# Linear attention and a two-layer feed-forward on one core: an earlier release for batch 1's loads, two tokens' transposes begun sooner, batch 2's exponentials placed behind more activations

## The chip, the cores and the metric

The kernel runs on one core of a Trainium2 chip. The metric is the device time of one execution in microseconds; times of several runs are given as a median. A profiled execution has a time of its own, and its span is the stretch from its first to its last instruction.

A core has TensorE (PE; its weight loads are shown as PEld), VectorE (DVE), ScalarE (ACT), GpSimd (POOL) and SyncE (SP), each running its own instructions in order and waiting on semaphores. SP issues most of the transfers, POOL the ones that change the type, and 16 DMA engines move the data of all queues. In the profile q1 is the queue fed by SP and q0 the one fed by POOL.

## The reference

```python
def _attn_ref(q, k, v):                       # 8 batches, 8 heads, 576 tokens, 64 wide
    q_s = exp(q - max(q, axis=-1)); q_s = q_s / sum(q_s, axis=-1)
    k_s = exp(k - max(k, axis=2));  k_s = k_s / sum(k_s, axis=2)
    kv = einsum('bhsd,bhse->bhde', k_s, v)
    return einsum('bhsd,bhde->bhse', q_s, kv)

x = attn_out.transpose(0, 2, 1, 3).reshape(4608, 512)
h = x @ w_in                                  # 512 x 2048
out = maximum(0.01 * h, h) @ w_out            # 2048 x 512, float32
```

## The kernel before

**Layout.** The attention of each batch is prepared on 128 partitions: heads come in two halves (`H0`, `H1`), and each partition holds nine rows (`R = 9`) of 64 values for each of four head pairs. For `k` the maximum over all tokens is taken on VectorE (`k_tree`, `k_allmax`), subtracted (`k_sub`) and exponentiated on ScalarE (`k_exp`); for `q` a maximum per row (`q_max`), a subtraction (`q_sub`), an exponential (`q_exp`), a sum (`q_sum`) and a scaling (`q_norm`). `v_cast` puts `v` into bfloat16. `kv` multiplies keys and values on TensorE, first heads of gg = 0, then of gg = 1; `kd_make` scales the result into a block-diagonal tile. The scaled `q` is turned, for batch 0 by transposes on TensorE (`q_transpose`, copied out by `q_keep`), for later batches by a DMA (`q_turn`, issued on SP). `attend` or `attend_x` multiplies the turned `q` with the `kd` tile, and a copy puts the product into `xT`, the input of the feed-forward.

**The feed-forward** runs over nine tiles of 512 tokens. For each of 16 column blocks j, `layer1` makes four matmuls into a PSUM tile `ph`, over the column blocks 0, 2, 1, 3 of `w_in` in this order, and `leaky` (ScalarE, line 470) writes the activation into `g_sb`. Then `layer2` (line 482) sums 16 matmuls for each of four groups of 128 tokens into `pout`, and `store` copies and sends it. Tile 0 takes 576 tokens instead of 512 and is split further. Its first 256 tokens come in halves: `begin(j)` makes the matmuls with column blocks 0 and 2 for j and j + 1, and line 682 the ones with 1 and 3; the remaining 320 tokens follow in one loop, and tile 0's `layer2` goes with j outermost, four token groups for each j. Six PSUM banks (`psB`) are handed out in turn to `ph`, `po`, `pkv`, `psum_qt` and others.

**Order.** All instruction streams are in the order of the program text. Preparation of later batches is put between matmuls by hand: `at(t, u, ...)` files functions under tile t and step u, and `run(t, u)` emits them there. In tile t ≥ 1 step j comes behind the `leaky` of block j (0 to 15), and steps 16 and up come behind every fourth matmul of `layer2`. `plan2` places batch 2 in tile 1 (lines 623 to 638), `plan` the later ones.

**Loads.** `w_in` comes in two halves of columns. Each is four DMAs on POOL's queue, in the order (gg, hp): gg chooses column blocks {0, 2} or {1, 3}, hp the partitions 0 to 63 or 64 to 127. `w_out` follows in six DMAs, also on POOL's queue, behind a gate: the copy on line 579 reads an element of the first half of batch 1's `k`, so POOL goes on only when that has landed. `k`, `q` and `v` of batch 1 are issued on SP (lines 576 to 578), and they are held: `hold_sync` (line 513) issues a small DMA on SP that reads some elements of `w_in_sb`, and SP doesn't come to the loads behind it before the transfer that writes these elements has landed. The elements lie in partition 64, column block 0, last 128 columns.

Of the kernel before, what the change touches and what calls it, by code (L numbers as in the profile page):

```python
# [25 lines left out]
def kernel(  # L26
# [9 lines left out]
    nc = tc.nc  # L36
# [3 lines left out]
    B, H, S, D = q.shape  # L40
    C = H * D
    T = B * S
    Cm, F = moe_w_in.shape
# [28 lines left out]
    def load(src, b, name, cuts):  # L72

        t = raw_pool.tile([P, HL, R, D], FP32, name=name, tag="raw")
        flat = src[b].rearrange("h s d -> (h s d)").rearrange(
            "(hl p r d) -> p hl r d", hl=HL, p=P, r=R
        )
        for hs, rs in cuts:
            nc.sync.dma_start(
                out=t[:, hs, rs].rearrange("p h r d -> p h (r d)"),  # L80
                in_=flat[:, hs, rs].rearrange("p h r d -> p h (r d)"),
            )
        return t

    ALLH, ALLR = slice(0, HL), slice(0, R)
# [28 lines left out]
    w_in_sb = w_pool.tile([P, NB, F], BF16)  # L114
# [29 lines left out]
    def k_begin(b):  # L144
        st[b]["ke"] = ke_pool.tile([P, R, HL, D], BF16, name="ke")
        st[b]["kmax"] = mx_pool.tile([P, HL, D], FP32, name="kmax")
        st[b]["kmaxT"] = mx_pool.tile([P, HL * D], FP32, name="kmaxT")
        st[b]["kall"] = mx_pool.tile([P, HL, D], FP32, name="kall")

    def k_tree(b, hs, steps=slice(0, 4)):  # L150
        n = hs.stop - hs.start
        ks = st[b]["k"][:, hs]
        if steps.start == 0:
            st[b]["t4"] = mx_pool.tile([P, HL, 4, D], FP32, name="t4")[:, 0:n]
        t4 = st[b]["t4"]
        t2, t1 = t4[:, :, 0:2], t4[:, :, 0]
        for o, i0, i1 in (
            (t4, ks[:, :, 0:4], ks[:, :, 4:8]),
            (t2, t2, t4[:, :, 2:4]),
            (t1, t1, t4[:, :, 1]),  # L160
            (st[b]["kmax"][:, hs], t1, ks[:, :, 8]),
        )[steps]:
            nc.vector.tensor_tensor(out=o, in0=i0, in1=i1, op=ALU.max)  # L163

    def k_allmax(b):


        nc.vector.transpose(
            out=st[b]["kmaxT"], in_=st[b]["kmax"].rearrange("p h d -> p (h d)")
        )  # L170
        m2 = small_pool.tile([P, CB, 2], FP32, name="m2")
        nc.vector.tensor_reduce(
            out=m2[:, :, 0],
            in_=st[b]["kmaxT"].rearrange("p (c j) -> p c j", j=32),
            axis=AX.X,
            op=ALU.max,
        )
        for a in range(4):
            o = a ^ 1
            nc.vector.tensor_reduce(  # L180
                out=m2[32 * o : 32 * o + 32, :, 1],
                in_=m2[32 * a : 32 * a + 32, :, 0:1],
                axis=AX.X,
                op=ALU.max,
            )
        m = small_pool.tile([P, CB], FP32, name="m")
        nc.vector.tensor_reduce(out=m, in_=m2, axis=AX.X, op=ALU.max)
        nc.vector.transpose(  # L188
            out=st[b]["kall"].rearrange("p h d -> p (h d)"),
            in_=m.unsqueeze(2).to_broadcast([P, CB, 32]),  # L190
        )

    def k_sub(eng, b, hs):
        ks = st[b]["k"][:, hs]
        n = hs.stop - hs.start
        eng.tensor_tensor(  # L196
            out=ks,
            in0=ks,
            in1=st[b]["kall"][:, hs].unsqueeze(2).to_broadcast([P, n, R, D]),
            op=ALU.subtract,  # L200
        )

    def k_exp(b, hs):
        nc.scalar.activation(  # L204
            out=st[b]["ke"][:, :, hs].rearrange("p r h d -> p h r d"),
            in_=st[b]["k"][:, hs],
            func=AF.Exp,
        )
# [10 lines left out]
    def q_begin(b):  # L219
        st[b]["qe"] = qe_pool.tile([P, R, HL, D], BF16, name="qe")  # L220
        if b == 0:
            for gg in range(2):
                st[b]["qT", gg] = qT_pool.tile([P, 2, R, L], BF16, name=f"qT{gg}", tag="qT")
# [42 lines left out]
    def q_exp(b, rs):  # L266
        nc.scalar.activation(  # L267
            out=st[b]["qe"][:, rs].rearrange("p r h d -> p h r d"),
            in_=st[b]["q"][:, :, rs],
            func=AF.Exp,  # L270
        )

    def q_sum(b, rs):
        n = rs.stop - rs.start
        qsum = small_pool.tile([P, n, HL], FP32, name="qsum")
        nc.vector.reduce_sum(out=qsum, in_=st[b]["qe"][:, rs], axis=AX.X)  # L276
        st[b]["qrec", rs.start] = qrec = small_pool.tile([P, n, HL], FP32, name="qrec")
        nc.vector.reciprocal(out=qrec, in_=qsum)

    def q_norm(b, rs):  # L280
        n = rs.stop - rs.start
        qes = st[b]["qe"][:, rs]
        nc.vector.tensor_tensor(  # L283
            out=qes,
            in0=qes,
            in1=st[b]["qrec", rs.start].unsqueeze(3).to_broadcast([P, n, HL, D]),
            op=ALU.mult,
        )
# [104 lines left out]
    def q_transpose(b, r0, n):  # L393
        ps = psB_pool.tile([P, NB, n, L], BF16, name="psum_qt", tag=BANK_TAG)
        for rr in range(n):
            for gg in range(2):
                nc.tensor.matmul(
                    ps[:, gg::2, rr],
                    lhsT=st[b]["qe"][:, r0 + rr, 2 * gg : 2 * gg + 2].rearrange(
                        "p h d -> p (h d)"  # L400
                    ),
                    rhs=ident,
                    is_transpose=True,
                    start=(rr == 0 and gg == 0),
                    stop=(rr == n - 1 and gg == 1),
                )
        st[b]["ps", r0] = ps

    def q_keep(eng, b, r0, n, ggs=(0, 1)):
        for gg in ggs:  # L410
            o, i = st[b]["qT", gg][:, :, r0 : r0 + n], st[b]["ps", r0][:, gg::2]
            if eng is nc.scalar:
                eng.copy(out=o, in_=i)
            else:
                eng.tensor_copy(out=o, in_=i)
# [20 lines left out]
    def q_turn(b, rs=ALLR):  # L436
        if rs.start == 0:
            st[b]["qX"] = qT_pool.tile([P, R * 2, P], BF16, name="qX", tag="qT")
        nc.sync.dma_start_transpose(
            out=st[b]["qX"][:, 2 * rs.start : 2 * rs.stop],  # L440
            in_=st[b]["qe"][:, rs].rearrange("p r h d -> p (r h d)"),
        )
# [50 lines left out]
    def at(t, u, *fns):  # L493
        while t > 0 and u >= 32:
            t, u = t + 1, u - 32
        hooks.setdefault((t, u), []).extend(fns)
# [16 lines left out]
    def hold_sync(i, src):  # L513
        nc.sync.dma_start(out=held[:, i], in_=src)
# [57 lines left out]
    q_norm(0, R1)  # L572


    hold_sync(0, w_in_sb[D : D + 1, 0, F - 128 : F])
    st[1]["k"] = load(k, 1, "k_raw", [(H0, ALLR), (H1, ALLR)])
    st[1]["q"] = load(q, 1, "q_raw", [(ALLH, ALLR)])
    st[1]["v"] = load(v, 1, "v_raw", [(ALLH, ALLR)])
# [44 lines left out]
    def plan2():  # L623
        b = 2
        at(1, 0, lambda: k_begin(b), lambda: q_begin(b), lambda: k_tree(b, ALLH))
        at(1, 3, lambda: k_allmax(b))
        at(1, 6, lambda: k_sub(nc.vector, b, H0), lambda: k_sub(nc.vector, b, H1))
        at(1, 9, lambda: k_exp(b, ALLH))
        for rs in XR:
            at(1, 9, lambda rs=rs: q_max(b, rs), lambda rs=rs: q_sub(nc.gpsimd, b, rs))  # L630
        at(1, 13, lambda: v_cast(nc.gpsimd, b, 0), lambda: v_cast(nc.gpsimd, b, 1))
        for i, rs in enumerate(XR):
            at(1, (13, 16)[i], lambda rs=rs: q_exp(b, rs), lambda rs=rs: q_sum(b, rs), lambda rs=rs: q_norm(b, rs))
            at(1, (15, 17)[i], lambda rs=rs: q_turn(b, rs))
        at(1, 21, lambda: kv(b))
        at(1, 22, lambda: kd_make(b))
        for i in range(8):
            at(1, 28 + i // 2, lambda i=i: attend_x(b, i % 4, XR[i // 4], nc.scalar))
# [20 lines left out]
    def begin(j):  # L659
        ph = psB_pool.tile([P, 2, 256], FP32, name="ph", tag=BANK_TAG)  # L660
        for i in range(2):
            layer1(j + i, ph[:, i], 0, 256, slice(0, 2), i == 0)
        begun.append(ph)
# [7 lines left out]
    q_norm(0, R2)  # L671
    for j in range(0, NF, 2):
        if j == 8:
            for jj in range(8, NF, 2):
                begin(jj)
            q_transpose(0, 4, 2)
            q_transpose(0, 6, 3)
            q_keep(nc.vector, 0, 4, 2)
            q_keep(nc.vector, 0, 6, 3)
        ph = begun.pop(0)  # L680
        for i in range(2):
            layer1(j + i, ph[:, i], 0, 256, slice(2, 4), i == 0, i == 1)
            if i == 1:
                leaky(g_sb[j // 2][:, :, 0:256], ph)
            run(0, j + i)
# [72 lines left out]
```

## Time and profile before

| | |
|---|---|
| median of 3 runs | 292.64 us (292.42 to 292.85) |
| profiled execution | 292.92 us |
| its span | 291.1 us |
| TensorE busy | 278.7 us, 96% of the span |
| VectorE, ScalarE, GpSimd busy | 148.5, 147.9, 86.0 us |
| granted TensorE clock | 1.000 |
| data moved by DMA | 46.35 MB |
| the held DMA's issue on SP | 21.07 us |
| tile 0's last `layer1` matmul ends, its `layer2` begins | 34.88 us, 35.55 us |

The busy time of an engine is the union of its instructions; for TensorE matmuls overlap each other in their records, since they are pipelined, and a gap between two records is shorter than the time that was lost. A timeline row gives start, duration, engine, line, operation and tiles of instructions of one kind in a row, and in brackets the idle time before them with what ended it. Issues of a DMA are listed with the time from issue to landing. Rows of a DMA queue give packets, megabytes and the time that its packets took as a share of 16 engines.

### The profile page before, as it was taken

Reading aid. Unit: us, or ns where it says so; the run is one execution under the profiler, and the core shown is the slowest. Engines: PE = TensorE matmul, PEld = TensorE weight load, DVE = VectorE, ACT = ScalarE, POOL = GpSimd, SP = SyncE. Lnnn points to the kernel's source line nnn. Section 1 sums busy time; section 2 is a strip of 40 time slices with the busy share of each in tenths; the row PEclk is TensorE's granted clock in tenths of the full one; section 3 lists DMA queues with packets and bytes.
Section 4 is the critical chain, followed back from the end, with each engine's and each line's share of the span. In section 5 each row is a group of like instructions: output and inputs, shape, how many; then the busy total and the mean of one; then the engine's idle time right before and its main releaser. Section 6 shows DMA issues by size and latency. Waiting matters only on the chain.

```text
span 291.1 us, 4248 instructions
## 1 busy us (share of the span) xinstructions
PE 278.7 (96%) x1620; PEld 138.5 (48%) x1646; DVE 148.5 (51%) x246; ACT 147.9 (51%) x273; POOL 86.0 (30%) x70
## 2 busy tenths in 40 slices
PE   8689899998999999999999999999999999999995
PEld 3268644453444445454444444554455444444443
DVE  3997693796890796289275546645541200110011
ACT  4976870658168506941684339533953066017400
POOL 4734560008039108603910391029200000000000
PEclk9999999999999999999999999999999999999999
DMA  7998999998649365963298139913141310131033
GB/s 258 311 205 302 282 194 212 398 283 312 130 94 360 133 125 108 372 173 85 68 351 233 36 73 330 275 36 72 38 81 36 74 36 1 36 77 34 0 70 76
DMA packets 38932, 46.35 MB, mean 159 GB/s; under 512 B 18304, under 2 KB 21632, under 8 KB 38912
## 3 DMA queue, kind: packets, MB, share of 16 engines
q1 hardware_dynamic: 35456, 41.75, 48.7%
q0 software_dynamic: 3296, 4.20, 8.3%
q8 instruction: 13, 0.21, 0.3%
q10 hardware_dynamic: 160, 0.13, 0.1%
q14 instruction: 7, 0.06, 0.1%
HBM read 36.70 MB, written 9.44 MB: 158 GB/s over the span
## 4 chain that ended last, share of the span: by engine, by line
PE 74%; issue 1%; ACT 0%; DVE 0%; ACTq 0%
PE pout L482 37%; PE ph L461 33%; PE pkv L298 2%; PE po L449 2%; ACT gj L470 0%; ACT xT L455 0%; DVE out_sb L476 0%; ACTq L470 0%
## 5 line engine op out<-in xcount | busy, mean ns | idle before, releaser
L482 PE MATMUL pout<-w_out_sb,gj 128*128 128x512 bf16 (+2 forms) x580 | 129.1, 373 | 2.9 <-DMA w_out_sb<-in_moe_w_out_dram 1.1
L461 PE MATMUL ph<-xT,w_in_sb 128*128 128x512 bf16 (+3 forms) x627 | 126.8, 357 | 1.9 <-DMA w_in_sb<-in_moe_w_in_dram 0.7
L470 ACT ACTIVATE gj<-ph 128x512 bf16<-128x512 f32 (+2 forms) x152 | 83.3, 581 | 56.8 <-PE ph L461 54.9
L461 PEld LDWEIGHTS <-w_in_sb 128*128 128x128 bf16 x640 | 62.2, 98 | 63.4 <-issue 2.3
L482 PEld LDWEIGHTS <-gj 128*128 128x128 bf16 x592 | 56.9, 98 | 65.4 <-issue 3.1
L476 DVE COPY out_sb<-pout 128x512 f32<-128x512 f32 (+1 forms) x34 | 22.7, 675 | 86.1 <-PE pout L482 82.6
L196 POOL TENSOR_TENSOR k_raw<-k_raw,kall 128x2304 f32<-128x2304 f32 x5 | 25.3, 5070 | 77.5 <-DVE kall L188 50.4
L455 ACT CAST xT<-po 128x320 bf16<-128x320 f32 (+1 forms) x54 | 18.8, 405 | 49.4 <-PE po L449 49.4
L259 POOL TENSOR_TENSOR q_raw<-q_raw,qmax 128x2304 f32<-128x2304 f32 (+3 forms) x10 | 29.7, 2977 | 23.3 <-DVE qmax L228 23.3
L276 DVE TENSOR_REDUCE qsum<-qe 128x36 f32<-128x2304 bf16 (+4 forms) x11 | 19.8, 1797 | 30.9 <-ACT qe L267 30.9
L204 ACT ACTIVATE ke<-k_raw 128x2304 bf16<-128x2304 f32 (+2 forms) x11 | 17.6, 1596 | 11.2 <-POOL k_raw L196 8.6
L283 DVE TENSOR_TENSOR qe<-qe,qrec 128x2304 bf16<-128x2304 bf16 (+4 forms) x12 | 21.9, 1826 | 0.4
L228 DVE TENSOR_REDUCE qmax<-q_raw 128x36 f32<-128x2304 f32 (+4 forms) x11 | 19.6, 1789 | 1.9 <-DMA q_raw<-in_q_dram 1.9
L267 ACT ACTIVATE qe<-q_raw 128x2304 bf16<-128x2304 f32 (+4 forms) x11 | 16.8, 1526 | 0.6 <-POOL q_raw L259 0.3
L216 POOL CAST vb<-v_raw 128x1152 bf16<-128x1152 f32 x13 | 14.6, 1153 | 0.0
L449 PE MATMUL po<-qX,kd 128*128 128x320 bf16 (+1 forms) x56 | 11.6, 286 | 0.3
L327 PE MATMUL pout<-zero 128*128 128x512 bf16 x27 | 9.2, 478 | 1.3 <-POOL zero L101 1.3
L163 DVE TENSOR_TENSOR t<-k_raw 128x1024 f32<-128x1024 f32 (+1 forms) x10 | 10.1, 1011 | 0.5 <-DMA k_raw<-in_k_dram 0.2
L163 DVE TENSOR_TENSOR t<-t 128x256 f32<-128x256 f32 (+2 forms) x20 | 9.6, 478 | 0.6
L476 ACT COPY out_sb<-pout 128x512 f32<-128x512 f32 (+1 forms) x3 | 1.6, 549 | 16.1 <-PE pout L482 16.1
L449 PEld LDWEIGHTS <-kd 128*128 128x128 bf16 x56 | 5.5, 98 | 6.8 <-issue 0.8
L298 PEld LDWEIGHTS <-ke 64*128 64x128 bf16 x252 | 7.1, 93 | 3.0 <-ACT gj L470 1.7
(61 smaller groups left out, 103.4 us busy)
## 6 DMA issues: line engine op xcount, KB each, us to landing
out_dram<-out_sb SPq DMA_DIRECT2D x70, 128.0 KB, 2.4
q_raw<-in_q_dram SPq DMA_DIRECT2D x7, 1152.0 KB, 8.1
v_raw<-in_v_dram SPq DMA_DIRECT2D x7, 1152.0 KB, 11.5
k_raw<-in_k_dram SPq DMA_DIRECT2D x6, 1152.0 KB, 5.7
k_raw<-in_k_dram SPq DMA_DIRECT2D x4, 576.0 KB, 4.8
w_in_sb<-in_moe_w_in_dram POOLq DMA_DIRECT2D x8, 256.0 KB, 7.1
v_raw<-in_v_dram SPq DMA_DIRECT2D x2, 576.0 KB, 7.4
w_out_sb<-in_moe_w_out_dram POOLq DMA_DIRECT2D x4, 256.0 KB, 11.1
```

Of the source, the lines that this page charges most:

```text
L163: nc.vector.tensor_tensor(out=o, in0=i0, in1=i1, op=ALU.max)
L196: eng.tensor_tensor(out=ks, in0=ks, in1=st[b]["kall"][:, hs].unsqueeze(2).to_broadcast([P, n, R, D]), op=ALU.subtract,)
L228: nc.vector.tensor_reduce(out=m, in_=st[b]["q"][:, :, rs], axis=AX.X, op=ALU.max)
L259: eng.tensor_tensor(out=qs, in0=qs, in1=st[b]["qmax", rs.start].unsqueeze(3).to_broadcast([P, HL, n, D]), op=ALU.subtract,)
L276: nc.vector.reduce_sum(out=qsum, in_=st[b]["qe"][:, rs], axis=AX.X)
L283: nc.vector.tensor_tensor(out=qes, in0=qes, in1=st[b]["qrec", rs.start].unsqueeze(3).to_broadcast([P, n, HL, D]), op=ALU.mult,)
L449: nc.tensor.matmul(ps.rearrange("p (r l) -> p r l", l=L), lhsT=kd2[b % 2][:, g], rhs=qX[:, gg, hh, rs])
L455: eng.copy(out=o, in_=ps)
L461: nc.tensor.matmul(ph, lhsT=w_in_sb[:, cb, j * P : (j + 1) * P], rhs=xT[:, XB[cb], c0 : c0 + n], start=(i == 0 and first), stop=(i == NB - ...
L470: nc.scalar.activation(out=o, in_=ph, func=AF.Prelu, alpha=LEAKY_SLOPE)
L476: copy(out=out_sb, in_=pout)
L482: nc.tensor.matmul(pout, lhsT=g_sb[j // 2][:, j % 2, tsub * P : (tsub + 1) * P], rhs=w_out_sb[:, j, os], start=(j == 0), stop=(j == NF - 1),)
```

## The change

Three edits.

- The held DMA reads its 128 elements from partition 0 instead of partition 64. Partition 0 is written by the first of the four transfers of w_in's second half, partition 64 by the second.
- In tile 0, when j reaches 8, the four transposes of batch 0's rows 4 and 5 come ahead of the sixteen matmuls of `begin(8)` to `begin(14)` instead of behind them. The copies on VectorE keep their order; in the program text the first of them stands ahead of the other six transposes now. PSUM banks go out in the new order.
- In tile 1, batch 2's `k_exp` comes behind block 12 instead of block 9; its first `q_exp` with `q_sum` and `q_norm` behind block 15 instead of 13, and the first `q_turn` at step 16 instead of 15. The second `q_exp` and `q_turn` stay at steps 16 and 17.

```diff
@@ -572,7 +572,7 @@
-    hold_sync(0, w_in_sb[D : D + 1, 0, F - 128 : F])
+    hold_sync(0, w_in_sb[0:1, 0, F - 128 : F])
     st[1]["k"] = load(k, 1, "k_raw", [(H0, ALLR), (H1, ALLR)])
     st[1]["q"] = load(q, 1, "q_raw", [(ALLH, ALLR)])
     st[1]["v"] = load(v, 1, "v_raw", [(ALLH, ALLR)])
@@ -625,13 +625,13 @@
         at(1, 6, lambda: k_sub(nc.vector, b, H0), lambda: k_sub(nc.vector, b, H1))
-        at(1, 9, lambda: k_exp(b, ALLH))
+        at(1, 12, lambda: k_exp(b, ALLH))
         for rs in XR:
             at(1, 9, lambda rs=rs: q_max(b, rs), lambda rs=rs: q_sub(nc.gpsimd, b, rs))
         at(1, 13, lambda: v_cast(nc.gpsimd, b, 0), lambda: v_cast(nc.gpsimd, b, 1))
         for i, rs in enumerate(XR):
-            at(1, (13, 16)[i], lambda rs=rs: q_exp(b, rs), lambda rs=rs: q_sum(b, rs), lambda rs=rs: q_norm(b, rs))
-            at(1, (15, 17)[i], lambda rs=rs: q_turn(b, rs))
+            at(1, (15, 16)[i], lambda rs=rs: q_exp(b, rs), lambda rs=rs: q_sum(b, rs), lambda rs=rs: q_norm(b, rs))
+            at(1, (16, 17)[i], lambda rs=rs: q_turn(b, rs))
         at(1, 21, lambda: kv(b))
@@ -671,11 +671,11 @@
     for j in range(0, NF, 2):
         if j == 8:
+            q_transpose(0, 4, 2)
             for jj in range(8, NF, 2):
                 begin(jj)
-            q_transpose(0, 4, 2)
+            q_keep(nc.vector, 0, 4, 2)
             q_transpose(0, 6, 3)
-            q_keep(nc.vector, 0, 4, 2)
             q_keep(nc.vector, 0, 6, 3)
         ph = begun.pop(0)
```

## The prediction

> **What bounds the kernel now.** I read the page first: engine shares, then the chain.
>
> ```profile
> PE 278.7 (96%) x1620; PEld 138.5 (48%) x1646; DVE 148.5 (51%) x246; ACT 147.9 (51%) x273; POOL 86.0 (30%) x70
> PE 74%; issue 1%; ACT 0%; DVE 0%; ACTq 0%
> ```
>
> TensorE sets the end. Only what shortens or lengthens its idle time counts, and 291.1 − 278.7 = 12.4 us of that is left, much of it in the start-up. The chain begins at 69.65 us: behind that point no piece but matmuls is longer than 0.6 us. So I took TensorE's timeline for the idle stretches ahead of it (start, duration, what, idle before).
>
> ```profile
> 21.19 1.91 PE L461 MATMUL ph<-xT,w_in_sb 128*128 128x256 bf16 x16 [0.73 <-DMA w_in_sb<-in_moe_w_in_dram]
> 22.94 0.72 PE L397 MATMUL psum_qt<-ident,qe 128*128 128x128 bf16 x10
> 23.50 1.04 PE L461 MATMUL ph<-xT,w_in_sb 128*128 128x256 bf16 x8
> 24.92 9.96 PE L461 MATMUL ph<-xT,w_in_sb 128*128 128x256 bf16 x72
> 35.55 1.89 PE L482 MATMUL pout<-w_out_sb,gj 128*128 128x512 bf16 x7 [0.68 <-DMA w_out_sb<-in_moe_w_out_dram]
> 37.86 5.34 PE L482 MATMUL pout<-w_out_sb,gj 128*128 128x512 bf16 x24 [0.42 <-DMA w_out_sb<-in_moe_w_out_dram]
> 65.67 2.97 PE L482 MATMUL pout<-w_out_sb,gj 128*128 128x512 bf16 x13
> 69.66 2.46 PE L482 MATMUL pout<-w_out_sb,gj 128*128 128x512 bf16 x10 [1.02 <-POOL q_raw L259]
> ```
>
> Four waits: for w_in at 21.19, twice for w_out, and one at 69.66. The change touches all four. A matmul's record outlasts its turn, so real losses are larger than the bracket. Second-layer matmuls last 0.38 and follow one another by 0.216 (the 24 at 37.86: (5.34 − 0.38)/23). Thus: w_out 0.83 (last L461 starts 34.58, the next could at 34.72) plus 0.58 (37.06 + 0.22 = 37.28 against 37.86), together 1.41. At 69.66: last start 68.26, the next could at 68.48; 1.18, and 0.13 more inside the next rows (ten matmuls there take 2.46, where 9 × 0.216 + 0.38 = 2.32), together 1.31.
>
> The page puts the last wait down to POOL. ScalarE's timeline says otherwise:
>
> ```profile
> 64.01 2.12 ACT L204 ACTIVATE ke<-k_raw 128x2304 bf16<-128x2304 f32 x1 [2.35 <-DVE k_raw L196]
> 66.04 1.82 ACT L470 ACTIVATE gj<-ph 128x448 bf16<-128x448 f32 x4
> 67.81 1.27 ACT L267 ACTIVATE qe<-q_raw 128x1280 bf16<-128x1280 f32 x1
> 68.99 0.96 ACT L470 ACTIVATE gj<-ph 128x448 bf16<-128x448 f32 x2
> ```
>
> ScalarE stands at batch 2's k_exp for 2.35 us with leaky 10 to 15 queued behind it, then puts q_exp ahead of leaky 14. That leaky ends near 69.5, and TensorE goes on at 69.66.
>
> **Hold (line 575).** The second half of w_in is four DMAs. Asked one by one, they give issue to landing:
>
> ```profile
> w_in_sb<-in_moe_w_in_dram POOLq DMA_DIRECT2D x1, 256.0 KB, 5.5
> w_in_sb<-in_moe_w_in_dram POOLq DMA_DIRECT2D x1, 256.0 KB, 7.1
> w_in_sb<-in_moe_w_in_dram POOLq DMA_DIRECT2D x1, 256.0 KB, 7.4
> w_in_sb<-in_moe_w_in_dram POOLq DMA_DIRECT2D x1, 256.0 KB, 8.0
> ```
>
> Issued at 13.36, 13.94, 14.53 and 15.11, they land at 18.9, 21.1, 21.9 and 23.1. Partition 64 of gg = 0 is the second, partition 0 the first. The hold (SP, 21.07 now) goes at about 18.87, so all four batch-1 loads issue 2.2 us sooner: k's first half at 19.5 for 21.74. k's landing opens line 579's gate on POOL (25.68), behind which stand the six w_out DMAs (first issue 26.28, landing 35.51). Nothing else is queued on SP meanwhile.
>
> The cost: k's first rows moved about 1.25 us after issue (from 22.95), so they now come from about 20.8, while w_in still moves. Two stretches show how queues share:
>
> ```profile
> q0 software_dynamic: 340, 0.63, 112.1%
> q1 hardware_dynamic: 259, 0.59, 57.8%
> q0 software_dynamic: 258, 0.25, 49.7%
> ```
>
> The first row is 16 to 19 us, w_in alone; the others are 31 to 34, where v and w_out rows go one for one. A load's row costs about 0.10 us of an engine (641 large ones in 26 to 30 on 16 engines). From 20.8 w_in has about 1 us left on most engines, but on one lagging engine its rows run to 22.9, 0.17 each: 12 of them. One for one, that engine carries 12 load rows in between, some 1.1 us (0.093 the median row). The fourth transfer then lands at 24.2. Bounds: 0 (the loads come behind the tail) and 3.2 (both halves of k, 32 rows an engine, ahead of it); I take 1.1, from the 259 against 258. The second transfer (21.1) may slip by 0.2; j = 8 hides that.
>
> TensorE needs the third and fourth at j = 8, line 682's cb 1 and 3 (23.50 now). From landing to matmul was 0.13 at 21.19, so j = 8 starts at 24.36: 0.86 late. Layer 1 to 34.88 has no idle, so layer 2 could begin at 34.72 + 0.86 = 35.58. k's first half lands near 24.5 rather than 25.56 (16 rows on the lagging engine, interleaved); w_out moves up with it by about 1.1, 35.5 to 34.4 and 37.8 to 36.7, ahead of TensorE at 35.6 and 37.3. Both waits go. Gain: 1.41 − 0.86 = 0.55.
>
> By a rule of the Trainium skill (DMA: Bandwidth & Descriptors, "Queues, rings and completion order") an SDMA engine drains a whole packet of typically 9 to 17 descriptors before it changes queue. The 259 against 258 rows speak for one-for-one here; what the rule would make of it is the second rival.
>
> **Transposes (line 676).** Four transposes of 0.055 (ten start from 22.94 to 23.44) move into the idle stretch ahead of 21.19; their qe was ready at 20.2 (L283). That is 0.22 off TensorE's order. By itself it would be lost at the w_out wait; here the late fourth transfer swallows it. VectorE's copies stay in order and find psum sooner; PSUM slots shift by one, and each tile is released before it is wanted (leaky 6 ends at 21.44; line 677 comes at 22.94). Counted at 0; 0.22 if the tail doesn't slip.
>
> **Batch 2's exponentials.** k_exp goes behind leaky 12 and q_exp behind leaky 15. Leaky 10 to 12 fit into the 2.35 us idle (blocks come every 0.77), so k_exp starts at 64.0 as before; leaky 13 to 15 follow by 67.5, and q_exp starts when its subtraction is done on POOL (67.8) as before. VectorE and SP keep their order: q_turn stays ahead of the same stores. TensorE reaches j = 13 at 68.26 and finds all written: 1.31 gone. What is late next is kv(2), for POOL's value casts:
>
> ```profile
> 69.58 2.24 POOL L216 CAST vb<-v_raw 128x1152 bf16<-128x1152 f32 x2
> 72.12 1.13 PE pkv L298 x36
> ```
>
> POOL's order is unchanged, ending 71.82. kv's second half starts near 72.57 now, would at 71.26, and must wait until about 71.92. Net 1.31 − 0.66 = 0.65 (bounds: 0 if the whole gain waits later, 1.31 if casts move up too). Later covers: kd_make ends 77.4 and q_turn's first part lands at 77.0, for attend_x at 79.2 less 0.65; VectorE's next copy waited 1.2 for TensorE. All of this starts from TensorE's end of tile 0, so the two gains add.
>
> **Sum.** 0.55 + 0 + 0.65 = 1.20. The profiled execution took 292.92 (span 291.1, 1.8 around it), 0.28 over the median of 292.64; 291.72 by it, 291.4 by the median.
>
> **Rivals.**
> No collision: the loads' rows come behind w_in's tail, or its lag is absent. j = 8 starts 0.22 early; w_out, up to 2.2 sooner, still comes first: 1.41 + 0.22 + 0.65 = 2.28, 290.4. For it: the lag hangs on one engine. Against: equal shares at 31 to 34. Chance 0.17.
>
> Slower, the loads cut in: k's rows run many at a time ahead of w_in's last. With all 32 per engine the fourth lands 3.2 late, at 26.3; j = 8 starts at 26.46, 2.96 late: 1.41 − 2.96 + 0.65 = −0.90, 293.5. It decides for slower once the fourth transfer is over 2.3 late (1.41 + 0.65 + the 0.24 from 23.26 to 23.50). With 16 rows, 1.6 late, 0.70 is still gained. Against: the one-for-one counts. Chance 0.14, of which 0.02 for the mild end.
> By the Trainium skill's rule (DMA: Bandwidth & Descriptors, same section) a turn of 9 to 17 descriptors would be 0.9 to 1.7 us here, an estimate at 0.10 a row: the mild end, unless turns repeat.
>
> The hold doesn't let w_out in sooner (k lands as late, since it shares): both w_out waits stay, the transposes' 0.22 drowns in them, 0.65 is left: 292.0. Chance 0.10.
>
> The exponentials' wait returns whole at kv(2) or attend_x: 0.55 left, 292.1. Chance 0.12.
>
> **How the numbers follow.** The forecast has 0.47. A measurement here tells about 0.2% (0.59 us) from no change. Faster by more: forecast and first rival, 0.64, and 0.10 of the last two, whose 0.65 and 0.55 lie at the edge: 0.74. Same: their other 0.12 and the mild cut-in's 0.02, 0.14. Slower: the cut-in past its point, 0.12. The range runs from 290.2, the first rival with 0.2 more (casts that move up too), to 292.9, which holds the last two and no change; left out are the cut-in and little besides.
>
> **What would show it.** Held's DMA near 18.9; the fourth w_in landing at about 24.2; an idle stretch of about 0.9 on TensorE ahead of j = 8, in place of both w_out waits; L482 of tile 0 starting near 35.6; none at j = 14 of tile 1, but about 0.6 inside kv(2). Wrong if the w_in wait grows past 2.3, if w_out's waits stay, or if kv(2) waits 1.3.

## The result and the profile after

The changed kernel takes 290.96 us (median of 6 runs, 290.80 to 291.12) against 292.63 us before (6 runs): 1.67 us less, ratio 0.9945 with a 95% interval of 0.9932 to 0.9957. Its profiled execution took 291.04 us with a span of 289.2, against 292.92 and 291.1, so the two traces differ by 1.9 us.

First the page of the changed kernel: TensorE's busy time hardly differs (some of its records were missing from the trace before), and the chain now passes through POOL's value casts.

```profile
PE 279.7 (97%) x1646; PEld 138.5 (48%) x1646; DVE 148.5 (51%) x246; ACT 148.2 (51%) x273; POOL 85.6 (30%) x70
PE 74%; POOL 1%; ACT 0%; DVE 0%; issue 0%
```

TensorE's timeline of the changed kernel, at the places of the four waits:

```profile
20.27 0.39 PE L397 MATMUL psum_qt<-ident,qe 128*128 128x128 bf16 x4
21.32 1.91 PE L461 MATMUL ph<-xT,w_in_sb 128*128 128x256 bf16 x16 [0.66 <-DMA w_in_sb<-in_moe_w_in_dram]
23.07 0.50 PE L397 MATMUL psum_qt<-ident,qe 128*128 128x128 bf16 x6
23.69 1.03 PE L461 MATMUL ph<-xT,w_in_sb 128*128 128x256 bf16 x8
34.91 7.07 PE L482 MATMUL pout<-w_out_sb,gj 128*128 128x512 bf16 x32
64.22 5.34 PE L482 MATMUL pout<-w_out_sb,gj 128*128 128x512 bf16 x24
69.55 0.69 PE L298 MATMUL pkv<-vb,ke 64*128 64x129 bf16 x18
70.64 0.69 PE L298 MATMUL pkv<-vb,ke 64*128 64x129 bf16 x18 [0.41 <-POOL vb L216]
```

Both w_out waits are gone: tile 0's layer 2 runs its first 32 matmuls without a break from 34.91, where it stood until 35.55 and again until 37.86. j = 8 starts at 23.69 instead of 23.50. The key-value product (kv) of batch 1 starts at 41.91 for 43.13, so tile 0 gives 1.22 us. In tile 1 the wait at j = 14 is gone (24 matmuls in 5.34, that is 23 × 0.216 + 0.38), and kv(2) is cut in two by a wait for the second cast. Tile 2's first matmuls start at 80.89 for 82.81: 1.92 in all, 0.70 of it from tile 1.

### The profile page after: what moved, and what is told of

Same layout as the page of the kernel before. It is cut to its first block, busy times and chain, and to the rows that moved or that the text cites. A ratio compares the mean times of both kernels' runs of the same rounds, so it can differ in the third digit from the quotient of the medians.

```text
span 289.2 us, 4274 instructions
## 1 busy us (share of the span) xinstructions
PE 279.7 (97%) x1646; PEld 138.5 (48%) x1646; DVE 148.5 (51%) x246; ACT 148.2 (51%) x273; POOL 85.6 (30%) x70
## 4 chain that ended last, share of the span: by engine, by line
PE 74%; POOL 1%; ACT 0%; DVE 0%; issue 0%
PE pout L482 37%; PE ph L461 34%; PE pkv L298 2%; PE po L449 2%; POOL vb L216 1%; ACT xT L455 0%; DVE out_sb L476 0%
## 5 line engine op out<-in xcount | busy, mean ns | idle before, releaser
L476 ACT COPY out_sb<-pout 128x512 f32<-128x512 f32 (+1 forms) x3 | 1.6, 543 | 15.6 <-PE pout L482 15.6
L298 PE MATMUL pkv<-vb,ke 64*128 64x129 bf16 x252 | 8.5, 216 | 0.4 <-POOL vb L216 0.4
```

The costliest lines, as they stand in the source:

```text
L298: nc.tensor.matmul(pkv[hh][:, gg, 0:129], lhsT=st[b]["ke"][rows, r, 2 * gg : 2 * gg + 2].rearrange("p h d -> p (h d)"), rhs=vb2[b % 2][row ...
L476: copy(out=out_sb, in_=pout)
```

## The experiments

Beside them the kernel before had medians of 292.4 to 292.7 and spread more than in the result (291.05 to 293.96). Differences are therefore taken from each kernel's ratio to the kernel before that ran beside it; the changed kernel's is 0.9945. The intervals reach 0.3 to 0.7 us to either side, so what is smaller is read from the traces. These start up to 0.5 us apart (w_in's second half is issued from 13.33 us in the changed kernel, from 13.36 before the change and from 13.83 in the latest), so a time in one trace can be compared with that in another only with this in mind. Diffs are against the kernel before for the first two, against the changed kernel for all others.

### The parts alone

The hold alone:

```diff
-    hold_sync(0, w_in_sb[D : D + 1, 0, F - 128 : F])
+    hold_sync(0, w_in_sb[0:1, 0, F - 128 : F])
```

> Only the hold on the first transfer; transposes and batch 2's exponentials as before. If the hold alone takes both w_out waits away (1.41 us) and pays only j = 8's delay (0.19 in the changed kernel): 292.6 - 1.2 = 291.4, layer 2 of tile 0 from 34.9 without a wait, and the wait of 1.3 at j = 14 of tile 1 still there. Rival, the transposes' 0.22 is part of the gain: 291.6, layer 2 from 35.1.

Measured: 291.88 us, ratio 0.9968 (0.9956 to 0.9980), a gain of 0.6 to 1.3. TensorE's timeline of this run:

```profile
35.03 7.07 PE L482 MATMUL pout<-w_out_sb,gj 128*128 128x512 bf16 x31
64.56 2.97 PE L482 MATMUL pout<-w_out_sb,gj 128*128 128x512 bf16 x13
68.56 2.46 PE L482 MATMUL pout<-w_out_sb,gj 128*128 128x512 bf16 x10 [1.03 <-POOL q_raw L259]
```

Layer 2 of tile 0 has no wait and the one of tile 1 is untouched. The interval holds both times that were expected; the trace parts them. The whole execution lies 0.2 us later from its start on (the matmuls ahead of 17 us), so 35.03 stands for the 34.9 expected, and the rival's 35.1 is out.

The exponentials alone (the three lines of `plan2`, nothing else):

> Only batch 2's exponentials moved. If q_exp ahead of leaky 14 was the wait: 1.31 gone at j = 14, about 0.65 of it back in the middle of kv(2), 292.6 - 0.65 = 291.95. Rival, the wait was POOL's subtraction, as the row of before names it: POOL's order is unchanged, so no gain, 292.6.

Measured: 292.02 us, ratio 0.9981 (0.9967 to 0.9994), a gain of 0.2 to 1.0. In its timeline the wait at j = 14 is gone though POOL's order is the same, and the split of kv(2) is there:

```profile
65.66 5.13 PE L482 MATMUL pout<-w_out_sb,gj 128*128 128x512 bf16 x23
70.77 0.69 PE L298 MATMUL pkv<-vb,ke 64*128 64x129 bf16 x18
71.86 0.69 PE L298 MATMUL pkv<-vb,ke 64*128 64x129 bf16 x18 [0.41 <-POOL vb L216]
```

The two ratios add to 0.32% + 0.19% = 0.51%, against 0.55% for the whole change.

The changed kernel without the sooner transposes:

```diff
-            q_transpose(0, 4, 2)
             for jj in range(8, NF, 2):
                 begin(jj)
-            q_keep(nc.vector, 0, 4, 2)
+            q_transpose(0, 4, 2)
             q_transpose(0, 6, 3)
+            q_keep(nc.vector, 0, 4, 2)
```

> The changed kernel with the transposes put back behind begin(8..14). If the late fourth transfer of w_in sets j = 8, they are worth nothing beside the sooner hold: 290.95, within 0.1 of the changed kernel. Rival, they are worth their 0.22: 291.2.

Measured: 291.18 us, ratio 0.9947 (0.9934 to 0.9960): the same as the changed kernel, though the interval is too wide to rule out the rival's 0.22. The trace tells more: TensorE waits at j = 8 for the fourth transfer (landed 23.41).

```profile
23.54 1.03 PE L461 MATMUL ph<-xT,w_in_sb 128*128 128x256 bf16 x8 [0.45 <-DMA w_in_sb<-in_moe_w_in_dram]
```

In this trace the second transfer was early and TensorE didn't wait for it. In the changed kernel it did, until 21.32; with the order of before, which took 2.31 from there to j = 8 (21.19 to 23.50), j = 8 could have started at 23.63, and the fourth transfer let it start at 23.69. So the transposes are worth nothing beside the sooner hold, but only by 0.06.

### What in the exponentials counts

Only `k_exp` moved, `q_exp` and `q_turn` back (hold and transposes as changed):

```diff
-            at(1, (15, 16)[i], lambda rs=rs: q_exp(b, rs), ...
-            at(1, (16, 17)[i], lambda rs=rs: q_turn(b, rs))
+            at(1, (13, 16)[i], lambda rs=rs: q_exp(b, rs), ...
+            at(1, (15, 17)[i], lambda rs=rs: q_turn(b, rs))
```

> The changed kernel, but q_exp and q_turn of batch 2 back at steps 13 and 15; k_exp stays behind block 12. If q_exp ahead of leaky 14 is what made TensorE wait: the wait at j = 14 is back, and the whole of the exponentials' 0.7 is lost, 291.65. Rival, the 2.35 us that ScalarE stood at k_exp were the cause: 290.95.

Measured: 291.78 us, ratio 0.9978 (0.9967 to 0.9989). TensorE's wait is back (1.03 between the records, until 68.47). ScalarE's timeline shows how: k_exp no longer stands idle, but q_exp waits for POOL with the leaky of blocks 14 and 15 behind it, and TensorE goes on only behind the first of these.

```profile
62.81 2.12 ACT L204 ACTIVATE ke<-k_raw 128x2304 bf16<-128x2304 f32 x1
64.84 0.53 ACT L470 ACTIVATE gj<-ph 128x448 bf16<-128x448 f32 x1
66.62 1.27 ACT L267 ACTIVATE qe<-q_raw 128x1280 bf16<-128x1280 f32 x1 [1.25 <-POOL q_raw L259]
67.80 0.96 ACT L470 ACTIVATE gj<-ph 128x448 bf16<-128x448 f32 x2
```

Only `q_exp` and `q_turn` moved, `k_exp` back at step 9:

```diff
-        at(1, 12, lambda: k_exp(b, ALLH))
+        at(1, 9, lambda: k_exp(b, ALLH))
```

> The changed kernel, but k_exp of batch 2 back at step 9; q_exp stays behind block 15. If q_exp was the cause: leaky 10 to 15 run on end behind k_exp and end at about 67.5, j = 15 of the first token group comes at most 0.3 late, which kv(2)'s wait for the casts swallows: 290.95 to 291.1; q_exp starts 0.9 later, and attend_x may wait 0.1. Rival, k_exp's standing is the cause: 291.65.

Measured: 291.02 us, ratio 0.9947 (0.9933 to 0.9960), the changed kernel's. ScalarE again stands 2.35 us at k_exp, and it costs nothing:

```profile
62.52 2.12 ACT L204 ACTIVATE ke<-k_raw 128x2304 bf16<-128x2304 f32 x1 [2.35 <-DVE k_raw L196]
64.55 2.70 ACT L470 ACTIVATE gj<-ph 128x448 bf16<-128x448 f32 x6
67.09 2.25 ACT L267 ACTIVATE qe<-q_raw 128x1280 bf16<-128x1280 f32 x2
```

So the move of `q_exp` did all of it, as far as ratios and traces tell; the move of `k_exp`, which removes the longer idle time, did nothing.

### What is late next: a faster version

The changed kernel with batch 2's value casts ahead of its query subtractions on POOL:

```diff
+        at(1, 8, lambda: v_cast(nc.gpsimd, b, 0), lambda: v_cast(nc.gpsimd, b, 1))
         for rs in XR:
             at(1, 9, lambda rs=rs: q_max(b, rs), lambda rs=rs: q_sub(nc.gpsimd, b, rs))
-        at(1, 13, lambda: v_cast(nc.gpsimd, b, 0), lambda: v_cast(nc.gpsimd, b, 1))
```

> The changed kernel with batch 2's two value casts ahead of its query subtractions on POOL (step 8 instead of 13 of tile 1). If POOL's second cast holds kv(2)'s second half (0.6 us), that is gone: 290.35, with kv(2) in one piece. Rivals: VectorE is slowed by casts that now lie beside its k chain and the time comes back at k_exp or attend_x, 290.95; or more, 291.2.

Measured: 290.56 us (4 runs), ratio 0.9922 (0.9909 to 0.9934). It is the lowest ratio of all; its interval just touches the changed kernel's, and the trace shows the forecast step. POOL was idle when the values landed, and kv(2) is in one piece:

```profile
58.97 2.24 POOL L216 CAST vb<-v_raw 128x1152 bf16<-128x1152 f32 x2 [11.80 <-DMA v_raw<-in_v_dram]
60.17 3.51 DVE L196 TENSOR_TENSOR k_raw<-k_raw,kall 128x1152 f32<-128x1152 f32 x2
69.56 1.20 PE L298 MATMUL pkv<-vb,ke 64*128 64x129 bf16 x36
```

The rival was right on one point: VectorE's two subtractions beside the casts take 3.51 us where they took 2.63. No time comes back from it; attend_x finds its data.

### How soon the hold may be

One theory was behind the forecast: loads that come while w_in still moves take turns with it, row for row. Four kernels put the hold on another transfer (the changed one has the first of the second half).

On the last of the first half:

```diff
-    hold_sync(0, w_in_sb[0:1, 0, F - 128 : F])
+    hold_sync(0, w_in_sb[D : D + 1, 1, 0:128])
```

> The changed kernel with the hold on the last transfer of w_in's first half (lands 17.4 for 18.7). If batch 1's loads and w_in's tail share the engines row by row: loads' rows come 1.3 sooner, the fourth transfer lands about 0.9 later (24.4), the second some 0.3 later; j = 8 at 24.5, nothing to win at w_out any more: 291.8. Rival, the loads' rows don't reach the engines before w_in's tail is out (they came at 21.6, 2.2 after issue): 290.95.

Measured: 291.20 us, ratio 0.9967 (0.9952 to 0.9982). SP issued k at 18.25 instead of 19.40, but k's first half landed at 24.87 (24.78 in the changed kernel), and the fourth w_in at 23.66 (23.55). The rival was right: nothing came sooner, and hardly anything got in the way. The ratio lies 0.2% above the changed kernel's with overlapping intervals; whether anything is lost is open.

On the third of the first half (`w_in_sb[0:1, 1, 0:128]`):

> The same with the hold on the third transfer of the first half (lands at 16.2), the loads issued from about 16.9, when all of w_in's second half has been issued. Theory, waiting behind what stands there: no cost, 291.0, first loads' rows at 21.5 again. Rival, one row each from 1.3 after issue (18.2): some 22 w_in rows an engine are left, the fourth transfer 2 us later, 293.

Measured: 292.27 us, ratio 0.9991 (0.9975 to 1.0008). Neither fits. k was issued at 17.55, the fourth w_in landed at 24.36, 9.0 us after its issue where the changed kernel has 8.5, and TensorE waited 0.66 for it, until 24.49.

On the first of the first half (`w_in_sb[0:1, 0, 0:128]`):

> The changed kernel with the hold on the first transfer of w_in's first half (lands at 14.1), so batch 1's loads are issued from about 14.8, beside the issues of w_in's second half (13.3 to 15.7) instead of long behind them. Theory, a transfer's rows wait behind the rows of the other queue that stand at the engines before they came: now the loads stand there as early as the second half, the second transfer lands 2 us or more later than 21.2 and the fourth 3 us or more later than 23.5: 294 or slower. Rival, loads' rows move only when w_in's queue is empty, however early they come: 291.0. Second rival, one row each from the start: the fourth 3.0 later (32 rows at 0.093), 293.9.

Measured: 293.45 us, ratio 1.0033 (1.0008 to 1.0058): slower than before. k was issued at 15.62, the second w_in landed at 21.99, the fourth at 26.43. From their issues that is 0.3 and 2.4 us later than in the changed kernel, so the theory was right that it is slow and put both too late, the second above all; the second rival's 293.9 lies near, but its turns didn't come from the start.

```profile
22.12 1.91 PE L461 MATMUL ph<-xT,w_in_sb 128*128 128x256 bf16 x16 [0.96 <-DMA w_in_sb<-in_moe_w_in_dram]
26.57 1.03 PE L461 MATMUL ph<-xT,w_in_sb 128*128 128x256 bf16 x8 [2.20 <-DMA w_in_sb<-in_moe_w_in_dram]
```

The packets of the two queues show when the loads moved. First the changed kernel, 19.4 to 21.4 us, in which k and q are issued (there is no row for q1); then 21.4 to 23.4:

```profile
q0 software_dynamic: 216, 0.40, 109.4%
q1 hardware_dynamic: 302, 0.60, 79.3%
q0 software_dynamic: 63, 0.09, 26.0%
```

Then the kernel with the hold on the first of the first half: 15.6 to 19 us, and 19.5 to 23.5.

```profile
q0 software_dynamic: 387, 0.71, 112.4%
q1 hardware_dynamic: 8, 0.00, 0.3%
q0 software_dynamic: 233, 0.43, 61.7%
q1 hardware_dynamic: 235, 0.53, 40.6%
```

Loads issued beside a busy w_in move nothing large for 3.7 us or so (15.62 to 19.32; 17.55 to 21.35 in the run before), and only then go row for row, 233 against 235. If w_in's rows run out on most engines first, at about 21.5, they start there: so in the changed kernel (issued 19.40, first large row 21.61) and with the hold on the last of the first half (18.25, 21.55). Before the change, with the engines nearly idle, it was 1.2 (21.74 to 22.95).

The last rows of w_in show the same on a single engine. Before the change they start 0.15 us apart (22.21, 22.36, 22.52, 22.67), with no load beside them. In the changed kernel they do so too (22.19, 22.34, 22.49, 22.65, 22.80), though loads move on the other engines by then: this engine took no load row in between. With the hold on the first of the first half they start 0.25 apart (24.58, 24.83, 25.09, 25.34), which leaves room for one load row of 0.10.

By a rule of the Trainium skill (DMA: Bandwidth & Descriptors, "Queues, rings and completion order") engines go round the queues and change by whole packets, typically of 9 to 17 descriptors. The second stretch agrees as far as both queues get equal turns; no run here shows turns of 9 to 17 rows. The first 3.7 us aren't in that rule, and what holds the rows isn't shown by these runs.

On the fourth of the second half, later than before (`w_in_sb[D : D + 1, 1, F - 128 : F]`):

> The changed kernel with the hold on the fourth transfer (lands at about 23.1). If w_out follows the hold one for one: loads and w_out come 2.1 later than before the change, both w_out waits grow by that in sum to 3.5, and only the exponentials' 0.65 is kept: 294.0. Rival, w_out waits for something else than the hold: 291.

Measured: 295.45 us, ratio 1.0100 (1.0083 to 1.0118). The theory was right in kind and short by about 1.5 us. w_out's first landed at 37.31 for 35.51, 1.8 later, and layer 2 started at 37.36, some 2.9 us after it could have; the theory had 3.5 in two waits. Then came a cost that was in neither expectation: TensorE ran at half clock. Its timeline:

```profile
37.36 8.75 PE L482 MATMUL pout<-w_out_sb,gj 128*128 128x512 bf16 x31 [2.73 <-DMA w_out_sb<-in_moe_w_out_dram]
```

Busy times by window, 34 to 38, 38 to 42 and 42 to 46 us (behind the length TensorE, its weight loads, VectorE, ScalarE, POOL, then the granted clock, the DMA share and GB/s):

```profile
34.00:38.00 4.00, 1.21 (x7) 0.60 (x7) 3.31 (x10) 2.23 (x5) 2.25 (x1) 1.00 1.18 253
38.00:42.00 4.00, 4.00 (x12) 1.51 (x11) 3.96 (x4) 4.00 (x4) 1.63 (x1) 0.57 1.25 207
42.00:46.00 4.00, 4.00 (x20) 1.67 (x17) 3.90 (x4) 1.30 (x2) 2.76 (x6) 1.00 1.29 179
```

The first 32 matmuls take 8.75 instead of 7.07, 1.7 more. In half-microsecond windows the clock is whole up to 38.0, 0.79 over 38.0 to 38.5, 0.50 from there to 41.5 and 0.80 up to 42.0: some 3.4 us at half speed, which is the 1.7. The trace has kv of batch 1 at 46.04, 2.9 later than before the change, where the theory had 2.1. So the clock more than makes up for what the theory lacked there. The rest of the 1.5 isn't explained: this trace is only 2.3 us longer than the one before the change, the medians' ratio gives 2.9.

## Why the prediction was right, and where its sizes were off

**The hold.** The benefit came as forecast: w_out comes sooner, both waits of together 1.41 go, and j = 8 pays. The price was off: 0.86 forecast, 0.19 measured. The step that failed is the 12 load rows between w_in's rows on the lagging engine: there were none. It rested on loads' rows coming from 20.8, 1.25 us after issue, taken from a stretch in which the engines were nearly idle, and on the one-for-one turns of 31 to 34 us, in which both queues had long been busy. In the changed kernel no load row moved ahead of 21.4, and on the engine with w_in's tail none before its last row. In this the first rival was right (the loads' rows come behind the tail); what it missed is that the fourth transfer is late all the same, by 0.42 instead of 1.1, which takes the 0.22 from it. So 1.41 − 0.19 = 1.22, between the forecast's 0.55 and the rival's 1.63.

Some 0.28 of the 0.42 lies between the last packet of w_in's queue and the landing: 0.59 us (22.96 to 23.55) for 0.31 (22.82 to 23.13). It was 0.50 to 0.59 in all six kernels with this hold and 0.31 to 0.35 in the three with a later one; what delays it isn't shown. The last packet's own time, 7.4 to 7.9 us after the fourth issue with this hold and 7.5 to 7.9 with a later one, spreads more than the rest of the 0.42.

The gain of w_out was mis-sized too, on the safe side: 1.1 sooner was forecast, 2.5 measured (33.03 for 35.51). k's first half landed only 0.8 sooner (24.78 for 25.56) and w_out was issued 0.9 sooner (25.36 for 26.28); the rest came between issue and landing, and its cause stays open. The landing times of the four transfers in the changed kernel, issued at 13.33, 13.91, 14.49 and 15.08, answer to those shown:

```profile
w_in_sb<-in_moe_w_in_dram POOLq DMA_DIRECT2D x1, 256.0 KB, 5.4
w_in_sb<-in_moe_w_in_dram POOLq DMA_DIRECT2D x1, 256.0 KB, 7.3
w_in_sb<-in_moe_w_in_dram POOLq DMA_DIRECT2D x1, 256.0 KB, 7.5
w_in_sb<-in_moe_w_in_dram POOLq DMA_DIRECT2D x1, 256.0 KB, 8.5
```

**The slower rival.** Loads that hold up w_in's tail exist and were priced about right: with the hold on the first of the first half the fourth transfer lands 10.85 us after its issue for 8.02 before, 2.8 late for 3.2. They did it row for row, though, not many at a time, and the full cost needs loads issued some 4 us sooner than the change's.

**The transposes.** Worth nothing, as forecast, and by the step forecast: the late fourth transfer sets j = 8. It does so by 0.06 only, where the forecast had 0.86; with an earlier transfer they would have counted.

**The exponentials.** 0.70 measured for 0.65, and the wait came back where the forecast put it, at the second cast (kv(2)'s second half at 70.64). The reading of ScalarE against the page's own naming of POOL was right, with one refinement: the experiments give all of it to `q_exp`, none to `k_exp`. POOL's subtraction is what q_exp waits for, so the page named the start of the chain, but the cure was in ScalarE's order.

**The sum.** 1.20 forecast, 1.67 by the medians, 1.92 by the traces. Of the traces' surplus of 0.72 the hold has 0.67 (1.22 for 0.55). The time, 290.96, lies about midway between the forecast's 291.4 and the first rival's 290.4, and the range held it because it took in that rival, not because the hold's price was right.

## What to carry to other kernels

An engine that takes instructions in order turns another engine's delay into a wait for everything queued behind: look for what stands behind the waiting instruction, and whether a consumer needs it first. The longest idle time is not the one that costs: here 2.35 us at k_exp cost nothing, and q_exp, which didn't stand idle at all before the change, made TensorE wait 1.3, and moving it gave 0.7. And when a transfer is let go sooner, price its onset from a stretch in which the engines are as busy as they will be, not from a quiet one. Of the places tried for the hold the best was in the middle: loads issued 1.8 us sooner than the change's, or 2.3 (as before the change) and 4.4 us later, lost time.

## What the runs showed of the hardware

A transfer issued while another queue keeps the DMA engines busy moved its first large rows 3.7 to 3.8 us after issue (15.62 to 19.32, 17.55 to 21.35), 1.2 us with the engines nearly idle (21.74 to 22.95), and only then shared row for row. The other way round, w_out's first large rows came 4.0 us after issue behind batch 1's loads (25.36 to 29.36 in the changed kernel).

TensorE's granted clock fell to half after an idle stretch of 2.73 us in front of tile 0's layer 2 (0.50 from 38.5 to 41.5 us), which cost 1.7 us more. It fell some 0.9 us after the work had begun again. In the trace of the kernel with the hold on the first of the first half, idle stretches of 0.96 and 2.20 us left the mean clock at 0.999; one other of its ten runs, the slowest, had 0.994, as the kernel with half clock has, and its waits aren't on record. The Trainium skill (TensorE: Matmul & The Clock Gate, "What's actually happening") puts the fall behind an idle window of about 3.4 us; here less than that was enough.
